# The second product of an MLP block as seven products of halves

## The chip, the cores and the metric

The kernel runs on one core of a Trainium2 chip. A core has a matrix engine (TensorE, PE in the profile; it writes its results to PSUM, eight banks of 128 partitions by 512 fp32 values), a vector engine (VectorE, DVE), a scalar engine (ScalarE, ACT), GpSimd (POOL), which here mainly issues loads, and a queue for DMA transfers (SyncE, SP). Each engine works through its own list of instructions in order and waits on semaphores for the others. The metric is the device time of one execution in microseconds (us). Before the change the median of three runs was 309.07 us (308.72 to 309.33).

## The reference

Retention attention over 8 sequences of 576 tokens with 8 heads of 64, followed by an MLP with a hard-swish:

```python
scores = scale * np.matmul(q, k.transpose(0, 1, 3, 2))
Dmat = np.where(rel >= 0, gamma ** rel, 0.0)
attn_out = np.matmul(scores * Dmat, v)
x = attn_out.transpose(0, 2, 1, 3).reshape(B * S, H * D)   # 4608 x 512
h = x @ w_in                                               # 512 x 2048
g = h * np.clip(h + 3.0, 0.0, 6.0) / 6.0
out = g @ w_out                                            # 2048 x 512, fp32 out
```

The change touches only the last line, for six of the nine blocks of tokens.

## The kernel before

**Tiling.** The 4608 tokens are cut into nine blocks of 512 (`MBLK`). Block `b` below 8 is the first 512 tokens of sequence `b`; block 8 gathers the last 64 tokens of each of the eight sequences. The attention works in pieces of 128 tokens: four main pieces per sequence, and a "rest" piece for the last 64 tokens of two sequences.

**GEMM1 of a block** (`gemm1`, `g1`, lines 402 to 410) has 16 units, one per 128 hidden features `fc`. A unit is four matmuls of 512 columns into one PSUM bank `ph`; ScalarE makes `u` from it (L409), and VectorE multiplies `u` and `ph` into `gt[:, fc, :]` (L410, f16). `gt` is the transposed `g` of the block: 128 partitions of features, 16 feature chunks, 512 tokens. There are two `gt` buffers.

**GEMM2 of a block** (`g2`, L460) also has 16 units: for each of four groups of 128 tokens (`mc`), four parts of four matmuls, with `gt` as weights and 512 columns of `wout16` moving. After the fourth part ScalarE copies the bank to `osb` (L464) and SP stores it (L445). The last group of the last block is done in two halves of 256 columns (`g2_halves`, L473).

**PSUM.** Four banks have the tag `ph` (GEMM1, GEMM2, and some attention tiles), two hold the scores `sc`, one `o`, one `u` of the states.

**The order around the change** is written out by hand (`manual_schedule`): the program text is the order of each engine. `put(units, steps)` emits the units of a GEMM and, after unit `j`, the work listed under `j`; -1 is ahead of the first. While block `kb` is in GEMM2 the attention of the pieces of block `kb + 1` is emitted in between:

- `step(ended, begun)` (lines 591 to 608): the inter-piece matmuls of the pieces that end (L325), the scores of the pieces that begin (L303 into `sc`, and L578 into two `ph` banks for the second one), then the products with v of those that end (L336, their results copied by ScalarE to `xt` at L342), and the state products of those that begin (L360). VectorE masks the scores (L307, L586) and advances the state (L373, or L376 and L377, giving `ts`); ScalarE copies `ts` into `tbd` with two copies (L389, L390).
- `ahead(c)`: transposes for the pieces of the block after the next, through SP (L288, and L294 after VectorE has scaled q and v at L293).

Blocks 2, 4 and 6 carry five pieces (one rest piece and four main pieces), blocks 1, 3 and 5 four, block 7 one. `AT` says after which units the steps come, by the number of pieces:

```python
AT = {1: (-1, 7), 4: (-1, 7, 12), 5: (-1, 3, 7, 11)}
```

GpSimd issues the loads of q, k, v (L91), six pieces ahead (`NBUF`); `load_until` in a step issues the next ones once buffers come free.

Of the kernel before, what the change touches and what calls it, by code (L numbers as in the profile page):

```python
# [10 lines left out]
FP32 = mybir.dt.float32  # L11
FP16 = mybir.dt.float16
ACTF = mybir.ActivationFunctionType
ALU = mybir.AluOpType
# [3 lines left out]
def kernel(  # L18
# [16 lines left out]
    nc = tc.nc  # L35
    B, H, S, D = q.shape
    NTOK, DM = out.shape
    DFF = moe_w_in.shape[1]
    P = 128
    NPAIR = H // 2  # L40
    HALF = P // 2
    NCC = DM // P
    NFC = DFF // P
    MBLK = 512
    NMB = NTOK // MBLK
    MAIN = MBLK
# [8 lines left out]
    for b in range(B):  # L55
# [3 lines left out]
        if b >= 2 and b % 2 == 0 or b == B - 1:  # L59
            j = (b - 1) // 2  # L60
# [2 lines left out]
    NP = len(pieces)  # L63
    lng = [float(np.log(1.0 - 2.0 ** (-5.0 - h))) for h in range(H)]

    def column_of(c):
        kind, b, i, _ = pieces[c]
        return b * MAIN + i * P if kind == "main" else B * MAIN + b * P

    const = ctx.enter_context(tc.tile_pool(name="const", bufs=1))  # L70
    big = ctx.enter_context(tc.tile_pool(name="big", bufs=1))
    nat = ctx.enter_context(tc.tile_pool(name="nat", bufs=6))
    work = ctx.enter_context(tc.tile_pool(name="work", bufs=3))
    psum = ctx.enter_context(tc.tile_pool(name="psum", bufs=1, space=bass.MemoryType.PSUM))
    ctx.enter_context(tc.manual_schedule())

    win16 = big.tile([P, NCC, DFF], FP16)
    wout16 = big.tile([P, NFC, DM], FP16)
    xt16 = big.tile([P, NCC, NTOK], FP16)

    loaded = {}
    EARLY = 4
    NBUF = 6

    def load(c):
# [29 lines left out]
    first = const.tile([P, 1], FP32)  # L115
    nc.scalar.activation(first, cb[:, 0:1], ACTF.Exp)
    lnr = const.tile([P, H], FP32)
    for h in range(H):
# [17 lines left out]
                            in1=gq[:, :, None].to_broadcast([P, H, P]), op=ALU.mult)  # L136
# [24 lines left out]
    for i in range(5):  # L161
        t = const.tile([P, NPAIR, P], FP16, name=f"tbd{i}")
        if i >= EARLY:
            nc.vector.memset(t, 0.0)
# [53 lines left out]
    def q_by_pe(c):  # L218
        q16, qk = loaded[c]["q16"], qk_of(c)
        pq = psum.tile([P, NPAIR, P], FP32, tag="ph", bufs=4, name=f"trq_{c}")  # L220
        for p in range(NPAIR):
            for h2 in range(2):
                r = slice(h2 * HALF, h2 * HALF + HALF)
                nc.tensor.matmul(pq[r, p, :], q16[:, 2 * p + h2, :], dq[:, 2 * p + h2, :],
                                 start=(p == 0), stop=(p == NPAIR - 1), skip_group_check=True)
        if c == EARLY - 1:
            for p in (0, 2):
# [22 lines left out]
    def out_last(c):  # L250
        before, qk = st[c]["before"], st[c]["qk"]
        at, vs = st[c]["at"], st[c]["vs"]
        g0 = column_of(c)
        halves = [psum.tile([P, NPAIR, P], FP32, tag="o", name=f"o_{c}"),
                  psum.tile([P, NPAIR, P], FP32, tag="ph", bufs=4, name=f"o2_{c}")]
        for i, o in enumerate(halves):
            for p in range(2):
                nc.tensor.matmul(o[:, p, :], tbd[before][:, 2 * i + p, :], qk[:, 0, 2 * i + p, :],
                                 start=(p == 0), stop=False, skip_group_check=True)
        for i, o in enumerate(halves):  # L260
            for p in range(2):
                for h2 in range(2):
                    r = slice(h2 * HALF, h2 * HALF + HALF)
                    nc.tensor.matmul(o[r, p, :], vs[:, 4 * i + 2 * p + h2, :],
                                     at[:, h2, 2 * i + p, :],
                                     start=False, stop=(p == 1), skip_group_check=True)
            nc.scalar.copy(xt16[:, 2 * i:2 * i + 2, g0:g0 + P], o[:, 0:2, :])  # L267

    def state_early(c):

# [60 lines left out]
    def intra(c, copy_later=False, more=False):  # L331
        o, at, vs = st[c]["o"], st[c]["at"], st[c]["vs"]
        for p in range(NPAIR):
            for h2 in range(2):
                r = slice(h2 * HALF, h2 * HALF + HALF)
                nc.tensor.matmul(o[r, p, :], vs[:, 2 * p + h2, :], at[:, h2, p, :],  # L336
                                 start=(st[c]["first"] and p == 0),
                                 stop=(p == NPAIR - 1 and not more), skip_group_check=True)
        g0 = column_of(c)

        def copy():
            nc.scalar.copy(xt16[:, :, g0:g0 + P], o)  # L342

        if copy_later:
            return copy
        copy()
# [50 lines left out]
    gts = {}  # L397

    def g1_mm(kb, ph, fc, dmcs):
        t0 = kb * MBLK  # L400
        for dmc in dmcs:
            nc.tensor.matmul(ph, win16[:, dmc, P * fc:P * fc + P], xt16[:, dmc, t0:t0 + MBLK],  # L402
                             start=(dmc == 0), stop=(dmc == NCC - 1))

    def g1_act(kb, ph, fc):
        if kb not in gts:
            gts[kb] = work.tile([P, NFC, MBLK], FP16, tag="gt16", bufs=2, name=f"gt16_{kb}")
        u = work.tile([P, MBLK], FP32, tag="moeu", bufs=3, name=f"u_{kb}_{fc}")
        nc.scalar.activation(u, ph, ACTF.Relu, bias=cb[:, 0:1], scale=1.0 / 6.0)  # L409
        nc.vector.scalar_tensor_tensor(out=gts[kb][:, fc, :], in0=u, scalar=1.0,  # L410
                                       in1=ph, op0=ALU.min, op1=ALU.mult)
# [8 lines left out]

    def g1_columns(kb, fc, ph, cols):

        t0 = kb * MBLK
        for dmc in range(NCC):
            nc.tensor.matmul(ph[:, cols], win16[:, dmc, P * fc:P * fc + P],  # L425
                             xt16[:, dmc, t0 + cols.start:t0 + cols.stop],
                             start=(cols.start == 0 and dmc == 0),
                             stop=(cols.stop == MBLK and dmc == NCC - 1),
                             skip_group_check=True)
        if cols.stop == MBLK:  # L430
            g1_act(kb, ph, fc)
# [10 lines left out]
    def store(kb, mc, cols, src):  # L442
        if kb < B:
            r0 = kb * S + P * mc
            nc.sync.dma_start(out[r0:r0 + P, cols], src)  # L445
        else:
            for i in range(2):
                r0 = (2 * mc + i) * S + MAIN
                queue = nc.scalar if i else nc.sync
                queue.dma_start(out[r0:r0 + HALF, cols], src[i * HALF:i * HALF + HALF])  # L450
# [3 lines left out]
    def g2(kb, mc, part):  # L454
        gt = gts[kb]
        if part == 0:
            pouts[kb, mc] = psum.tile([P, DM], FP32, tag="ph", bufs=4, name=f"pout_{kb}_{mc}")
        pout = pouts[kb, mc]
        for fc in range(4 * part, 4 * part + 4):
            nc.tensor.matmul(pout, gt[:, fc, P * mc:P * mc + P], wout16[:, fc, :],  # L460
                             start=(fc == 0), stop=(fc == NFC - 1))
        if part == 3:
            osb = work.tile([P, DM], FP32, tag="osb", bufs=4, name=f"osb_{kb}_{mc}")
            nc.scalar.copy(osb, pout)  # L464
            store(kb, mc, slice(0, DM), osb)

    def g2_halves(kb, mc):
        gt = gts[kb]
# [60 lines left out]
    def unit1(kb, f0):  # L529
        return lambda: g1(kb, f0)  # L530

    def unit2(kb, mc, part):
        return lambda: g2(kb, mc, part)
# [76 lines left out]
    def put(units, steps):  # L610

        for do, *which in steps.get(-1, ()):
            do(*which)
        for j, unit in enumerate(units):
            unit()
            run_later(1)
            for do, *which in steps.get(j, ()):
                do(*which)

    def of_block(kb):  # L620
        return list(range(last_of[kb - 1] + 1, last_of[kb] + 1)) if kb < NMB else []

    def gemm1(kb, steps):

        units = {0: [lambda: g1_first(kb)]}.get(kb, [])
        done = {0: 2, 1: 4}.get(kb, 0)
        put(units + [unit1(kb, f) for f in range(done, NFC)], steps)

    load_until(EARLY - 1 + NBUF)
    gemm1(0, {9: [(fill_gq,)]})
    order = [(mc, part) for part in range(4) for mc in range(3)] + [(3, part) for part in range(4)]
    put([unit2(0, mc, part) for mc, part in order],
        {3: [(first_step, 3)], 6: [(make_mask_rest,)], 9: [(first_step, 4)],
         11: [(first_step, 5)], 13: [(first_step, 6)], 14: [(first_step, 7), (transpose_k, 8)],
         15: [(transpose_k, 9)]})

    banks = [g1_bank(1, fc) for fc in range(4)]
    done, last = slice(0, 3 * P), slice(3 * P, MBLK)  # L640
# [4 lines left out]
    for fc, cols in ((2, done), (0, last), (1, last), (3, done), (2, last), (3, last)):  # L645
# [3 lines left out]

    gemm1(1, {0: [(transpose_q, 9)], 1: [(transpose_k, 10)],  # L650
              4: [(transpose_q, 10)], 5: [(transpose_k, 11)], 8: [(transpose_q, 11)]})
    AT = {1: (-1, 7), 4: (-1, 7, 12), 5: (-1, 3, 7, 11)}
    for kb in range(1, NMB - 1):
        mine, next_ = of_block(kb + 1), of_block(kb + 2)
        pairs = [mine[i:i + 2] for i in range(0, len(mine), 2)]
        steps = {}
        for j, ended, begun in zip(AT[len(mine)], [[]] + pairs, pairs + [[]]):
            steps.setdefault(j, []).append((step, ended, begun))
        for j, c in enumerate(next_, start=16 - len(next_)):
            steps.setdefault(j, []).append((ahead, c))  # L660
        put([unit2(kb, mc, part) for mc in range(MBLK // P) for part in range(4)], steps)
        gts.pop(kb)
        gemm1(kb + 1, {})
    for mc in range(MBLK // P - 1):
        for part in range(4):
            g2(NMB - 1, mc, part)
# [31 lines left out]
```

## Time and profile before

| | |
|---|---|
| median of three runs | 309.07 us (308.72 to 309.33) |
| profiled execution, first to last instruction (its span) | 309.9 us; the profile gives no other time for it |
| TensorE busy | 298.6 us, 2238 matmuls |
| VectorE busy | 185.2 us |
| ScalarE busy | 174.3 us |
| GpSimd busy | 109.0 us |
| GEMM2 matmuls of 512 columns (L460) | 560, 379 ns each from start to modelled end |
| GEMM2 matmuls of 256 columns (L473) | 32, 272 ns |
| block 4, GEMM2 with five pieces | 166.85 to 185.43 us |
| block 5, GEMM2 with four pieces | 199.34 to 216.91 us |
| block 7, GEMM2 with one piece | 263.30 to 278.14 us |

Matmuls are pipelined: the duration of one runs from its start to its modelled end, and the next starts earlier, so the rate is read from starts. A group's row in the profile gives its line in the kernel, engine, operation, tiles, shapes, count, then busy time and the mean of one, then the idle time of the engine ahead of it and what ended most of that. In a timeline each row is: start, duration of the merged group, engine, line, operation, tiles, shapes, count, and in brackets the idle time before it and who ended it. PEclk is the granted TensorE clock, 1.00 being full speed.

### The profile page before, as it was taken

The numbers are of one execution on the slowest core, as the hardware profiler recorded it, in microseconds if no ns is written. First come the engines' busy times: TensorE is split into PE (matmuls) and PEld (weight loads), VectorE is DVE, ScalarE is ACT, GpSimd is POOL, SyncE is SP. The second block draws the span as 40 slices with busy tenths as digits, with TensorE's granted clock in tenths as the row PEclk, the third lists the DMA queues.
The fourth block names the chain that finished last, engine by engine and source line by source line (L and its number), as shares of the span: only waits on it lengthen the run. The fifth ranks groups of instructions, "written<-read, shape, count | busy, mean of one in ns | idle before, by whom it ended". The sixth has DMA issues, their size and how long they took to land.

```text
span 309.9 us, 5776 instructions
## 1 busy us (share of the span) xinstructions
PE 298.6 (96%) x2238; PEld 150.2 (48%) x2238; DVE 185.2 (60%) x308; ACT 174.3 (56%) x301; POOL 109.0 (35%) x135
## 2 busy tenths in 40 slices
PE   5969998999999999999999999999999999999994
PEld 2634445644554554445544644455445544444443
DVE  4728616798657782885578746857688347307700
ACT  5528537685457463854475637644774567227611
POOL 8973568456522392035433650158000000000000
PEclk9779999999999999999999999999999999999999
DMA  9999999999999899629999999199930120011022
GB/s 71 144 199 203 190 146 197 130 152 148 156 173 111 110 153 174 122 17 157 149 136 114 125 167 160 18 134 151 141 87 36 68 68 2 34 68 36 1 68 68
DMA packets 153163, 35.51 MB, mean 115 GB/s; under 512 B 143792, under 2 KB 148656, under 8 KB 153136
## 3 DMA queue, kind: packets, MB, share of 16 engines
q0 software_dynamic: 117264, 18.36, 84.1%
q1 hardware_dynamic: 35472, 16.26, 26.5%
q10 hardware_dynamic: 400, 0.52, 0.5%
q8 instruction: 17, 0.28, 0.4%
q14 instruction: 10, 0.08, 0.1%
HBM read 36.70 MB, written 9.44 MB: 149 GB/s over the span
## 4 chain that ended last, share of the span: by engine, by line
PE 90%; POOL 4%; DMA 2%; ACT 2%; DVE 1%; issue 0%; POOLq 0%; ACTq 0%
PE ph L402 39%; PE pout L460 39%; PE o L336 3%; DMA qv<-in_v_dram 2%; POOL qv L91 2%; PE sc L303 2%; PE o L325 2%; PE u L360 1%; POOL kn L91 1%; PE pout L473 1%; PE sc L578 1%; PE ph L425 1%; ACT qk L216 0%; POOL vs L202 0%; ACT xt L342 0%
## 5 line engine op out<-in xcount | busy, mean ns | idle before, releaser
L410 DVE SCALAR_TENSOR_TENSOR gt<-u,ph 128x512 f16<-128x512 f32 x144 | 98.1, 687 | 67.4 <-ACT u L409 66.7
L460 PE MATMUL pout<-wout,gt 128*128 128x512 f16 x560 | 126.0, 379 | 0.0
L402 PE MATMUL ph<-xt,win 128*128 128x512 f16 x560 | 123.0, 380 | 0.5 <-ACT xt L267 0.3
L409 ACT ACTIVATE u<-ph,cb 128x512 f32<-128x512 f32 x144 | 98.3, 687 | 26.4 <-PE ph L402 25.2
L402 PEld LDWEIGHTS <-win 128*128 128x128 f16 x560 | 54.9, 98 | 66.9 <-issue 1.6
L460 PEld LDWEIGHTS <-gt 128*128 128x128 f16 x560 | 52.7, 98 | 60.8
L91 POOL DMA_DIRECT2D kn<-in_k_dram x40 | 34.4, 864 | 93.0 <-PE u L360 71.5
L464 ACT COPY osb<-pout 128x512 f32<-128x512 f32 x35 | 20.5, 586 | 48.9 <-PE pout L460 48.6
L307 DVE TENSOR_TENSOR at<-sc,mask_wide 128x1024 f16<-128x1024 f32 x19 | 23.2, 1222 | 27.2 <-PE sc L303 27.1
L91 POOL DMA_DIRECT2D qv<-in_q_dram x40 | 34.4, 866 | 5.6 <-DMA wout<-in_moe_w_out_dram 3.3
L91 POOL DMA_DIRECT2D qv<-in_v_dram x40 | 34.8, 876 | 2.9 <-DMA wout<-in_moe_w_out_dram 1.7
L389 ACT COPY tbd<-ts 64x256 f16<-64x256 f16 x28 | 11.3, 404 | 32.7 <-DVE ts L373 16.9
L342 ACT CAST xt<-o 128x512 f16<-128x512 f32 x35 | 19.4, 589 | 6.8 <-PE o L336 4.5
L293 DVE TENSOR_TENSOR vs<-qv,gqv 128x1024 f16<-128x1024 f16 x28 | 17.9, 685 | 2.9 <-DMA qv<-in_v_dram 2.9
L586 DVE TENSOR_TENSOR at<-sc,mask_wide 128x512 f16<-128x512 f32 x24 | 15.4, 681 | 0.0
L336 PE MATMUL o<-at,vs 128*64 128x128 f16 x280 | 12.4, 225 | 1.1 <-ACT xt L342 0.9
L390 ACT COPY tbd<-ts 64x256 f16<-64x256 f16 x28 | 11.2, 402 | 0.4
L336 PEld LDWEIGHTS <-vs 128*64 128x64 f16 x280 | 8.9, 111 | 4.4 <-DVE vs L202 2.1
L376 DVE TENSOR_TENSOR ta<-u,ts 128x256 f32<-128x256 f32 x21 | 8.7, 415 | 3.1 <-PE u L360 3.1
L377 DVE TENSOR_TENSOR ts<-ta,gc 128x256 f16<-128x256 f32 x21 | 8.9, 425 | 1.7
L303 PE MATMUL sc<-qk 64*128 64x128 f16 x184 | 9.4, 222 | 0.6 <-ACT qk L230 0.6
L325 PEld LDWEIGHTS <-tbd 128*128 128x128 f16 x112 | 7.0, 98 | 4.0
(70 smaller groups left out, 117.5 us busy)
## 6 DMA issues: line engine op xcount, KB each, us to landing
out_dram<-osb SPq DMA_DIRECT2D x32, 256.0 KB, 4.2
kn<-in_k_dram POOLq DMA_DIRECT2D x32, 128.0 KB, 4.4
qv<-in_q_dram POOLq DMA_DIRECT2D x32, 128.0 KB, 4.9
qv<-in_v_dram POOLq DMA_DIRECT2D x32, 128.0 KB, 5.8
wout<-in_moe_w_out_dram POOLq DMA_DIRECT2D x4, 512.0 KB, 14.7
win<-in_moe_w_in_dram POOLq DMA_DIRECT2D x3, 512.0 KB, 12.1
win<-in_moe_w_in_dram POOLq DMA_DIRECT2D x2, 256.0 KB, 8.1
kn<-in_k_dram POOLq DMA_DIRECT2D x8, 64.0 KB, 4.8
```

The source lines that it names most:

```text
L91: nc.gpsimd.dma_start(dst[p0:p0 + n], src[b, :, s0:s0 + n, :].rearrange("h s d -> s h d"))
L293: nc.vector.tensor_tensor(out=vs, in0=loaded[c]["qv"], in1=gqv, op=ALU.mult)
L303: nc.tensor.matmul(sc[:, h2, p, :], qk[r, 1, p, :], qk[r, 0, p, :], start=True, stop=True)
L307: later.append(lambda: nc.vector.tensor_tensor(out=at.rearrange("t a b s -> t (a b) s"), in0=sc.rearrange("t a b s -> t (a b) s"), in1=mas ...
L336: nc.tensor.matmul(o[r, p, :], vs[:, 2 * p + h2, :], at[:, h2, p, :], start=(st[c]["first"] and p == 0), stop=(p == NPAIR - 1 and not more ...
L342: nc.scalar.copy(xt16[:, :, g0:g0 + P], o)
L402: nc.tensor.matmul(ph, win16[:, dmc, P * fc:P * fc + P], xt16[:, dmc, t0:t0 + MBLK], start=(dmc == 0), stop=(dmc == NCC - 1))
L409: nc.scalar.activation(u, ph, ACTF.Relu, bias=cb[:, 0:1], scale=1.0 / 6.0)
L410: nc.vector.scalar_tensor_tensor(out=gts[kb][:, fc, :], in0=u, scalar=1.0, in1=ph, op0=ALU.min, op1=ALU.mult)
L460: nc.tensor.matmul(pout, gt[:, fc, P * mc:P * mc + P], wout16[:, fc, :], start=(fc == 0), stop=(fc == NFC - 1))
L464: nc.scalar.copy(osb, pout)
L586: nc.vector.tensor_tensor(out=at[:, h2], in0=banks[h2], in1=mask[:, None, :].to_broadcast([P, NPAIR, P]), op=ALU.mult)
```

## The change

For blocks 2 to 7 the product of `g` (512 x 2048) and `w_out` (2048 x 512) is split in two along tokens, features and output columns, and the eight products of halves are replaced by seven, with sums of halves on both sides (the scheme known from Strassen and Winograd, with nested sums).

- **Sums of `w_out`** (`tw1` to `tw4`, 128 x 8 x 256, f16) are made once by VectorE during GEMM2 of block 0, after units 5 to 8.
- **Sums of `g`** (`s1` to `s4`, 128 x 8 x 256, f16) are made by VectorE for every block. `s1` and `s2` are made in pieces during GEMM1, whose units now go in the order 0, 8, 1, 9, ... ; their last parts stand ahead of GEMM2, `s3` and `s4` after its units 3 and 4.
- **GEMM2** has 14 units: products 1, 2, 6, 5, 7, 3, 4, each for two groups of 128 tokens, eight matmuls of 256 columns per unit.
- **Results.** Three `ph` banks are used. Bank `b` accumulates products 1, 6, 7 and 4 in turn, and is copied to SBUF by ScalarE after 1, 6 and 7; the next product is added to what stands in it. Bank `c` does so with 5 and 3. Bank `a` holds product 2. VectorE adds two of the four output quarters, GpSimd one, ScalarE copies the fourth. Each half of 256 tokens is stored by one DMA of 512 KB.
- **Order.** `AT` has a second table for these blocks, for 14 units, and with five pieces the single one now comes first. `ahead` ends at unit 12 of 14 where it ended at 15 of 16.
- **Buffers.** One `gt` buffer in place of two; `xt` is one tile per block, two in turn, in place of one for all tokens.

```diff
+    SEVEN = 2
-            gts[kb] = work.tile([P, NFC, MBLK], FP16, tag="gt16", bufs=2, name=f"gt16_{kb}")
+            gts[kb] = work.tile([P, NFC, MBLK], FP16, tag="gt16", bufs=1, name=f"gt16_{kb}")
...
+    def combine_wout(i):
+        one, other = {1: (b12, b11), 2: (b22, tw[1]), 3: (b22, b12), 4: (b21, tw[2])}[i]
+        nc.vector.tensor_tensor(out=tw[i], in0=one, in1=other, op=ALU.subtract)
...
+    def sum_of(kb, i, q0, q1):
...
+        gt, sm, q = gts[kb], sums[kb], slice(q0, q1)
+        r = slice(half_k + q0, half_k + q1)
+        one, other, op = {1: (gt[:, q, hi], gt[:, r, hi], ALU.add),
+                          2: (sm[1][:, q], gt[:, q, lo], ALU.subtract),
+                          3: (gt[:, q, lo], gt[:, q, hi], ALU.subtract),
+                          4: (gt[:, r, lo], sm[2][:, q], ALU.subtract)}[i]
+        nc.vector.tensor_tensor(out=sm[i][:, q], in0=one, in1=other, op=op)
...
+    def product(kb, which, tt):
+        my, gt, sm = seven[kb], gts[kb], sums[kb]
+        chain, first, left, right = {
+            1: ("b", True, gt[:, lo_k, lo], b11),
+            6: ("b", False, sm[2], tw[2]),
+            7: ("b", False, sm[3], tw[3]),
+            4: ("b", False, gt[:, hi_k, hi], tw[4]),
+            2: ("a", True, gt[:, hi_k, lo], b21),
+            5: ("c", True, sm[1], tw[1]),
+            3: ("c", False, sm[4], b22)}[which]
+        if chain not in my:
+            my[chain] = psum.tile([P, 2, half_n], FP32, tag="ph", bufs=4, name=f"{chain}_{kb}")
+        for k in range(half_k):
+            nc.tensor.matmul(my[chain][:, tt], left[:, k, P * tt:P * tt + P], right[:, k, :],
+                             start=(first and tt == 0 and k == 0),
+                             stop=(k == half_k - 1), skip_group_check=True)
+
+    def gather(kb, which):
+        my = seven[kb]
+        if which in (1, 6, 7, 5):
+            my[which] = work.tile([P, 2, half_n], FP32, tag=f"part{which}", bufs=1,
+                                  name=f"part{which}_{kb}")
+            nc.scalar.copy(my[which], my["c" if which == 5 else "b"])
+        if which == 2:
+            my["lo"] = work.tile([P, 2, DM], FP32, tag="osb2", bufs=3, name=f"olo_{kb}")
+            nc.vector.tensor_tensor(out=my["lo"][:, :, lo_n], in0=my[1], in1=my["a"], op=ALU.add)
+        if which == 7:
+            my["hi"] = work.tile([P, 2, DM], FP32, tag="osb2", bufs=3, name=f"ohi_{kb}")
+            nc.gpsimd.tensor_tensor(out=my["hi"][:, :, hi_n], in0=my[7], in1=my[5], op=ALU.add)
+        if which == 3:
+            nc.vector.tensor_tensor(out=my["lo"][:, :, hi_n], in0=my[6], in1=my["c"], op=ALU.add)
+            store2(kb, 0, my["lo"])
+        if which == 4:
+            nc.scalar.copy(my["hi"][:, :, lo_n], my["b"])
+            store2(kb, 1, my["hi"])
...
+        return [unit(which, tt) for which in (1, 2, 6, 5, 7, 3, 4) for tt in range(2)]
...
-    AT = {1: (-1, 7), 4: (-1, 7, 12), 5: (-1, 3, 7, 11)}
+    AT = {False: {1: (-1, 7), 4: (-1, 7, 12), 5: (-1, 3, 7, 11)},
+          True: {1: (-1, 5), 4: (-1, 5, 12), 5: (-1, 1, 5, 12)}}
+    within = {4: [(1, 0, 2)], 8: [(1, 2, 4)], 10: [(2, 0, 4)], 12: [(1, 4, 6)]}
+    behind = {-1: [(1, 6, 8), (2, 4, 8)], 3: [(3, 0, 8)], 4: [(4, 0, 8)]}
...
+        single = len(mine) % 2 if by_seven else 0
+        pairs = [mine[:1]] * single + [mine[i:i + 2] for i in range(single, len(mine), 2)]
+        if by_seven:
+            for j, which in behind.items():
+                steps[j] = [(sum_of, kb, *w) for w in which]
...
-        for j, c in enumerate(next_, start=16 - len(next_)):
+        for j, c in enumerate(next_, start=(13 if by_seven else 16) - len(next_)):
```

More of the change, by code (lines that the diff above doesn't have):

```diff
@@ L64, with place_of @@
     lng = [float(np.log(1.0 - 2.0 ** (-5.0 - h))) for h in range(H)]
-    def column_of(c):
+    def place_of(c):
         kind, b, i, _ = pieces[c]
-        return b * MAIN + i * P if kind == "main" else B * MAIN + b * P
+        return (b, i * P) if kind == "main" else (B, b * P)
     const = ctx.enter_context(tc.tile_pool(name="const", bufs=1))
@@ L72 @@
     nat = ctx.enter_context(tc.tile_pool(name="nat", bufs=6))
+    xpool = ctx.enter_context(tc.tile_pool(name="xpool", bufs=2))
     work = ctx.enter_context(tc.tile_pool(name="work", bufs=3))
@@ L78, with xt_of @@
     wout16 = big.tile([P, NFC, DM], FP16)
-    xt16 = big.tile([P, NCC, NTOK], FP16)
+    xts = {}
+    def xt_of(kb):
+        if kb not in xts:
+            if kb == B:
+                xts[kb] = big.tile([P, NCC, MBLK], FP16, name="xt_rest")
+            else:
+                xts[kb] = xpool.tile([P, NCC, MBLK], FP16, tag="xt", name=f"xt_{kb}")
+        return xts[kb]
     loaded = {}
     EARLY = 4
+    SEVEN = 2
     NBUF = 6
@@ L252, in out_last @@
         at, vs = st[c]["at"], st[c]["vs"]
-        g0 = column_of(c)
+        kb, g0 = place_of(c)
         halves = [psum.tile([P, NPAIR, P], FP32, tag="o", name=f"o_{c}"),
@@ L266, in out_last @@
                                      start=False, stop=(p == 1), skip_group_check=True)
-            nc.scalar.copy(xt16[:, 2 * i:2 * i + 2, g0:g0 + P], o[:, 0:2, :])
+            nc.scalar.copy(xt_of(kb)[:, 2 * i:2 * i + 2, g0:g0 + P], o[:, 0:2, :])
     def state_early(c):
@@ L338, in intra @@
                                  stop=(p == NPAIR - 1 and not more), skip_group_check=True)
-        g0 = column_of(c)
+        kb, g0 = place_of(c)
         def copy():
-            nc.scalar.copy(xt16[:, :, g0:g0 + P], o)
+            nc.scalar.copy(xt_of(kb)[:, :, g0:g0 + P], o)
         if copy_later:
@@ L399, in g1_mm @@
     def g1_mm(kb, ph, fc, dmcs):
-        t0 = kb * MBLK
         for dmc in dmcs:
-            nc.tensor.matmul(ph, win16[:, dmc, P * fc:P * fc + P], xt16[:, dmc, t0:t0 + MBLK],
+            nc.tensor.matmul(ph, win16[:, dmc, P * fc:P * fc + P], xt_of(kb)[:, dmc, :],
                              start=(dmc == 0), stop=(dmc == NCC - 1))
@@ L421, in g1_columns @@
     def g1_columns(kb, fc, ph, cols):
-        t0 = kb * MBLK
         for dmc in range(NCC):
             nc.tensor.matmul(ph[:, cols], win16[:, dmc, P * fc:P * fc + P],
-                             xt16[:, dmc, t0 + cols.start:t0 + cols.stop],
+                             xt_of(kb)[:, dmc, cols],
                              start=(cols.start == 0 and dmc == 0),
@@ L465, in g2 @@
             store(kb, mc, slice(0, DM), osb)
+    half_k, half_t, half_n = NFC // 2, MBLK // 2, DM // 2
+    lo_k, hi_k = slice(0, half_k), slice(half_k, NFC)
+    lo, hi = slice(0, half_t), slice(half_t, MBLK)
+    lo_n, hi_n = slice(0, half_n), slice(half_n, DM)
+    tw = {i: big.tile([P, half_k, half_n], FP16, name=f"tw{i}") for i in range(1, 5)}
+    b11, b12 = wout16[:, lo_k, lo_n], wout16[:, lo_k, hi_n]
+    b21, b22 = wout16[:, hi_k, lo_n], wout16[:, hi_k, hi_n]
+    def combine_wout(i):
+        one, other = {1: (b12, b11), 2: (b22, tw[1]), 3: (b22, b12), 4: (b21, tw[2])}[i]
+        nc.vector.tensor_tensor(out=tw[i], in0=one, in1=other, op=ALU.subtract)
@@ new lines @@
+    sums = {}
+    def sum_of(kb, i, q0, q1):
+        if kb not in sums:
+            sums[kb] = {j: work.tile([P, half_k, half_t], FP16, tag=f"s{j}", bufs=1,
+                                     name=f"s{j}_{kb}") for j in range(1, 5)}
+        gt, sm, q = gts[kb], sums[kb], slice(q0, q1)
[5 more added lines that the diff above has]
+        nc.vector.tensor_tensor(out=sm[i][:, q], in0=one, in1=other, op=op)
@@ new lines @@
+    seven = {}
+    def product(kb, which, tt):
[14 more added lines that the diff above has]
+                             stop=(k == half_k - 1), skip_group_check=True)
@@ L467, in g2_halves, with store2, gemm2_seven, unit @@
+    def store2(kb, i, src):
+        r0 = kb * S + half_t * i
+        nc.sync.dma_start(out[r0:r0 + half_t, :].rearrange("(t p) n -> p t n", p=P), src)
+    def gemm2_seven(kb):
+        seven[kb] = {}
+        def unit(which, tt):
+            def do():
+                product(kb, which, tt)
+                if tt == 1:
+                    gather(kb, which)
+            return do
+        return [unit(which, tt) for which in (1, 2, 6, 5, 7, 3, 4) for tt in range(2)]
     def g2_halves(kb, mc):
@@ L625, in gemm1 @@
         units = {0: [lambda: g1_first(kb)]}.get(kb, [])
-        done = {0: 2, 1: 4}.get(kb, 0)
-        put(units + [unit1(kb, f) for f in range(done, NFC)], steps)
+        if kb < SEVEN or kb == NMB - 1:
+            rest = range({0: 2, 1: 4}.get(kb, 0), NFC)
+        else:
+            rest = [f for q in range(half_k) for f in (q, q + half_k)]
+        put(units + [unit1(kb, f) for f in rest], steps)
     load_until(EARLY - 1 + NBUF)
@@ L633 @@
     order = [(mc, part) for part in range(4) for mc in range(3)] + [(3, part) for part in range(4)]
[L634 to L637, printed above, removed]
+    steps = {3: [(first_step, 3)], 6: [(make_mask_rest,)], 9: [(first_step, 4)],
+             11: [(first_step, 5)], 13: [(first_step, 6)],
+             14: [(first_step, 7), (transpose_k, 8)], 15: [(transpose_k, 9)]}
+    for j, i in zip((5, 6, 7, 8), (1, 2, 3, 4)):
+        steps.setdefault(j, []).append((combine_wout, i))
+    put([unit2(0, mc, part) for mc, part in order], steps)
     banks = [g1_bank(1, fc) for fc in range(4)]
@@ L651 @@
               4: [(transpose_q, 10)], 5: [(transpose_k, 11)], 8: [(transpose_q, 11)]})
-    AT = {1: (-1, 7), 4: (-1, 7, 12), 5: (-1, 3, 7, 11)}
+    AT = {False: {1: (-1, 7), 4: (-1, 7, 12), 5: (-1, 3, 7, 11)},
+          True: {1: (-1, 5), 4: (-1, 5, 12), 5: (-1, 1, 5, 12)}}
+    within = {4: [(1, 0, 2)], 8: [(1, 2, 4)], 10: [(2, 0, 4)], 12: [(1, 4, 6)]}
+    behind = {-1: [(1, 6, 8), (2, 4, 8)], 3: [(3, 0, 8)], 4: [(4, 0, 8)]}
     for kb in range(1, NMB - 1):
+        by_seven = kb >= SEVEN
         mine, next_ = of_block(kb + 1), of_block(kb + 2)
-        pairs = [mine[i:i + 2] for i in range(0, len(mine), 2)]
+        single = len(mine) % 2 if by_seven else 0
+        pairs = [mine[:1]] * single + [mine[i:i + 2] for i in range(single, len(mine), 2)]
         steps = {}
-        for j, ended, begun in zip(AT[len(mine)], [[]] + pairs, pairs + [[]]):
+        if by_seven:
+            for j, which in behind.items():
+                steps[j] = [(sum_of, kb, *w) for w in which]
+        for j, ended, begun in zip(AT[by_seven][len(mine)], [[]] + pairs, pairs + [[]]):
             steps.setdefault(j, []).append((step, ended, begun))
-        for j, c in enumerate(next_, start=16 - len(next_)):
+        for j, c in enumerate(next_, start=(13 if by_seven else 16) - len(next_)):
             steps.setdefault(j, []).append((ahead, c))
-        put([unit2(kb, mc, part) for mc in range(MBLK // P) for part in range(4)], steps)
+        put(gemm2_seven(kb) if by_seven else
+            [unit2(kb, mc, part) for mc in range(MBLK // P) for part in range(4)], steps)
         gts.pop(kb)
-        gemm1(kb + 1, {})
+        gemm1(kb + 1, {j: [(sum_of, kb + 1, *w) for w in which] for j, which in within.items()}
+              if SEVEN <= kb + 1 < NMB - 1 else {})
     for mc in range(MBLK // P - 1):
```

## The prediction

> **What bounds the kernel now.** I read the page first: the busy line, the chain that ended last, the costliest groups.
>
> ```profile
> PE 298.6 (96%) x2238; PEld 150.2 (48%) x2238; DVE 185.2 (60%) x308; ACT 174.3 (56%) x301; POOL 109.0 (35%) x135
> ...
> PE 90%; POOL 4%; DMA 2%; ACT 2%; DVE 1%; issue 0%; POOLq 0%; ACTq 0%
> ...
> L460 PE MATMUL pout<-wout,gt 128*128 128x512 f16 x560 | 126.0, 379 | 0.0
> ...
> L464 ACT COPY osb<-pout 128x512 f32<-128x512 f32 x35 | 20.5, 586 | 48.9 <-PE pout L460 48.6
> ```
>
> TensorE is the bound: 96% busy, 90% of the chain, and no idle time ahead of L460. The edit takes TensorE columns away and gives VectorE and ScalarE work, so two questions decide: what is a 256-column matmul worth, and do two engines at 60% and 56% stay out of TensorE's way? The last block answers the first, since it has both shapes (timeline, TensorE alone: start, us, count).
>
> ```profile
> 291.95 10.52 PE L460 MATMUL pout<-wout,gt 128*128 128x512 f16 x48
> 302.31 3.66 PE L473 MATMUL pout<-wout,gt 128*128 128x256 f16 x32
> ```
>
> 48 wide matmuls take 302.31-291.95 = 10.36 us, 216 ns each. The 32 narrow ones, each with new weights, take 3.66 less the last one's own 0.272, over 31 starts: 109 ns. So the weight load stays hidden at half width. For the second question I read the timeline of one GEMM2 phase, block 5's, which starts with the scores at S = 199.34.
>
> ```profile
> 199.34 0.40 PE L303 MATMUL sc<-qk 64*128 64x128 f16 x8
> ...
> 200.26 7.08 PE L460 MATMUL pout<-wout,gt 128*128 128x512 f16 x32
> ...
> 200.77 1.22 DVE L307 TENSOR_TENSOR at<-sc,mask_wide 128x1024 f16<-128x1024 f32 x1
> ...
> 201.90 0.41 DVE L373 TENSOR_TENSOR ts<-u,gc 128x256 f16<-128x256 f32 x1
> 202.24 1.28 DVE L586 TENSOR_TENSOR at<-sc,mask_wide 128x512 f16<-128x512 f32 x2
> ...
> 203.88 0.42 DVE L377 TENSOR_TENSOR ts<-ta,gc 128x256 f16<-128x256 f32 x1
> ...
> 204.34 0.41 ACT L389 COPY tbd<-ts 64x256 f16<-64x256 f16 x1 [1.17 <-DVE ts L377]
> 204.75 0.40 ACT L390 COPY tbd<-ts 64x256 f16<-64x256 f16 x1
> ...
> 205.18 0.59 ACT L464 COPY osb<-pout 128x512 f32<-128x512 f32 x1
> ...
> 207.18 0.39 PE L325 MATMUL o<-qk,tbd 128*128 128x128 f16 x4
> ```
>
> The first output bank is complete at 200.26 + 16 x 0.216 = 203.7, but its copy runs at 205.18: ScalarE works in order, and the state copies ahead of it wait for ts, the end of a step's VectorE work. Today that costs nothing, as TensorE goes on in another bank. In the new scheme TensorE itself waits for that copy.
>
> **TensorE's saving.** Per block 64 x 0.2158 = 13.81 us become 112 x 0.1093 = 12.24: 1.57 less. The three phase types last, from their first scores to the next GEMM1, 18.58 us (five pieces; 166.85 to 185.43), 17.56 (four; 199.34 to 216.91) and 14.84 (one; 263.30 to 278.14). With attention costed by the same rows the phases without a wait would be 16.87 (one step's pairing also changes), 15.97 and 13.16. Six blocks: 3 x 1.71 + 2 x 1.59 + 1.68 = 10.0 us.
>
> **VectorE's new work.** Sums are two-input f16 operations inside SBUF. The nearest row is L293 (128x1024, 685 ns, 0.60 from start to start), and L202 (128x512, 419); so 0.42, 0.69 and 0.685 + 0.533 = 1.22 for 512, 1024 and 2048 elements. The upper bound is one element per cycle, as L135 shows (1.226 for 1024, one input repeated): 0.69, 1.22, 2.29. I take the lower: the sums' rows are contiguous over 256 elements as L293's are. The Trainium skill's "VectorE: DVE Perf Modes" (What auto-detection actually checks) asks for 16-bit types with step one; L293's 685 ns agrees, and no run here shows the strided case yet.
>
> In GEMM1 a VectorE unit is 0.69 of 0.863 us, so the four pieces of sums there (1.9 us) fit; their largest backlog is about 0.35 us, and a bank has about 1.0 to spare: nothing. The four sums of halves of w_out in block 0 (4.6 us) fall where VectorE waits 8.32 us for the scores; the last w_out load lands near 41.9, so they end near 45.4, just as L307 starts at 45.53: nothing, at worst 0.3.
>
> **Four-piece phases (3 and 5), times after S.** GEMM1's last gt is written at 1.52 (200.16 + 0.69). Then the last parts of s1 and s2, one dependent on the other, delay the first mask from 1.43 to 2.74. Masks and states keep their own row distances, so the second ts ends at 6.27 (204.30 - 199.34 + 1.31). ScalarE: two state copies to 7.12, then the copy of product 1's bank to 7.74. TensorE: scores and updates 0.92, products 1 and 2 to 4.42, and product 6 may not start before 7.78: **3.36 us idle**. Behind the copy hangs VectorE's queue: add of a and product 1 (0.59 effective, as L586), s3 and s4 (1.14 each), and only at 10.65 the second pair's mask; its states end at 14.76 (the step's rows, 207.94 to 212.09, are 4.1 us). ScalarE: state copies to 15.6, then the copy of product 5 to 16.22. Product 3 starts at 16.26 where TensorE, even after waiting 0.7 for a bank, stood ready at 15.4. Products 3 and 4 and the last step: 16.26 + 3.50 + 1.11 = 20.87. The xt copies then have one unit (0.875) to hide in instead of three and need 0.96 + 0.05 (214.19 + 1.07 - 214.31): 0.14 more. End 21.01 against 17.56: +3.45.
>
> **Five-piece phases (2, 4 and 6).** The single piece comes first; step 1 needs the one sc bank for the next scores, and its mask ends at 2.74 + 1.22 = 3.96, while TensorE is there at 2.3: 1.7 idle. Then VectorE's queue: masks and states to 7.94, add 8.53, s3 and s4 to 10.81, masks and states to 14.92; ScalarE's state copies to 15.77, product 5's copy to 16.38. Product 3 waits 1.65 for it. End: 16.42 + 3.50 + 1.11 + 0.14 = 21.17 against 18.58: +2.59.
>
> **Phase 7** has one piece; every copy is early, -1.68.
>
> ScalarE loses four output copies a block (0.586 each, L464) and gains five of that size; VectorE gains two adds (0.68 each, as L586) and the sums. In the phases above these are counted where they stand in the queues; their share of busy time plays no part.
>
> Sum: 3 x 2.59 + 2 x 3.45 - 1.68 = +13.0 us.
>
> **Queues and the rest.** SP: the transposes begin at unit 8 of 14 with one store among them that waits for the add of product 3, and ten of them at 1.3 us still end some 7 us before the next phase. POOL's add (1.15 by L202 on POOL) stands behind loads; only a store waits for it, with three output buffers. One gt buffer costs nothing: TensorE has read the old one before the first new bank is full.
>
> **The clock.** The trace shows what gaps do (one-us windows, TensorE: us, busy, granted clock, DMA):
>
> ```profile
> 5.00:6.00 1.00, 0.65 (x5) 1.00 2.07 132
> 6.00:7.00 1.00, 0.21 (x8) 1.00 2.29 146
> 7.00:8.00 1.00, 0.64 (x14) 1.00 2.31 147
> 8.00:9.00 1.00, 1.00 (x17) 0.79 2.25 143
> 9.00:10.00 1.00, 1.00 (x14) 0.50 2.06 131
> ```
>
> After three us about half idle, with no gap over 1.14 us, the clock is at 0.50 for three us. A gap of 3.36 us should do that in each four-piece phase. It doubles product 6 and the step after it, up to 1.7 us, of which VectorE's lead over the next scores (10.22 against 10.65) and the wait before product 3 take some: +1.0 each (bounds 0 and 1.7), 2.0 in all. The 1.7 us gaps of the five-piece phases leave a stretch half busy with dense matmuls; I take no drop.
>
> The Trainium skill's "TensorE: Matmul & The Clock Gate" (Part 1: The HAM clock gate) ties the drop to a whole idle window of about 3.4 us. By that rule 3.36 us would not do and the sum would stay at +13.0; the trace shows a drop without such a window.
>
> Total +15.0. The profiled span, 309.9, is 0.8 above the median of the runs, 309.07; the difference goes onto the median: **324.1 us**.
>
> **Rivals.**
> - *No clock drop*: +13.0, 322.1.
> - *Drops in the five-piece phases too*: after the first gap about 0.9 (product 2 comes late to the add), after the second up to 1.65 straight on the end: 3 x 2.55 = 7.7 more, 331.8. For it: the windows above. Against: those held small matmuls with longer pauses.
> - *Sums at one element per cycle*: (0.27 + 0.53) + 2 x 1.07 = 2.9 us more per phase in VectorE's queue, five phases: 322.1 + 14.7 = 336.8. Against: L293.
> - *Faster: the copy of the gathered bank is in time.* If ScalarE got to product 1's copy at 2.9 (bank full) instead of 7.1, and the adds and sums cleared likewise, only 10.0 less remains: 299.1. It decides where the waits come to less than 1.6 us a phase; in the row above a copy already runs 1.3 us late behind the states with no sums in the queue, which speaks against it.
>
> **Numbers.** 324.1: 0.42; 322.1: 0.25; 331.8: 0.19; 336.8: 0.08; 299.1: 0.05; 0.01 for anything near no change. Two runs here differ by up to 0.2%, about what can be told from no change. Range 317 to 335: it holds the first three cases, and small errors in VectorE's distances (5% of 13 us in five phases, 3.3 us).
>
> **What would show it.** Product matmuls 109 ns apart; product 6 in phases 3 and 5 waiting about 3.4 us for ScalarE's copy, which follows two state copies; in 2, 4 and 6 the second scores waiting 1.7 us for VectorE; product 3 waiting 0.8 to 1.7 us for the copy of product 5; phases of 21 to 22 us; sums of 1.22 us; a granted clock below 1 in the new phases. I am wrong if ScalarE's copies come out of this order, if sums cost double, or if the clock drops on every gap.

## The result and the profile after

| | before | after |
|---|---|---|
| median of four runs | 309.2 us (308.72 to 311.68) | 324.86 us (322.44 to 326.01) |
| profiled execution: span, time | 309.9 us; 311.7 us if the same 1.8 lies around it as after (the highest of the four runs took 311.68) | 324.2 us; 326.01 us |
| ratio | | 1.0473, 95% interval 1.0404 to 1.0541 |

The kernel is 4.7% slower. The page of the changed kernel, the busy line and the chain that ended last by engine and by line:

```profile
PE 293.4 (90%) x2526; PEld 179.6 (55%) x2526; DVE 225.0 (69%) x372; ACT 177.5 (55%) x307; POOL 116.7 (36%) x141
...
PE 68%; DVE 17%; ACT 6%; POOL 3%; issue 2%; DMA 2%; DVEq 0%; POOLq 0%; ACTq 0%
PE ph L412 38%; PE pout L469 11%; PE b L520 7%; PE c L520 4%; DVE at L318 4%; DVE at L679 4%; DVE s L502 4%; PE o L347 2%; DMA qv<-in_v_dram 2%; POOL qv L102 2%; DVE ts L388 2%; DVE ta L387 2%; DVE gt L420 1%; ACT u L419 1%; ACT part L530 1%
```

TensorE is busy for 5 us less and still the kernel takes longer: 17% of the chain is now VectorE's and 6% ScalarE's, where they had 1% and 2%. The waits of TensorE name the places (engine, line, for whom: total us, times, longest):

```profile
PE b L520 <- ACT part L530: 6.1, 2, 3.1
PE c L520 <- ACT part L530: 5.4, 5, 1.7
PE sc L314 <- DVE at L318: 4.2, 3, 1.4
PE c L520 <- ACT xt L353: 3.5, 5, 0.7
```

The first is product 6 in phases 3 and 5, the second product 3 in five phases, the third the scores in phases 2, 4 and 6, the fourth the bank of product 5. In phase 4, which starts with the scores at S = 173.66, the second scores and product 3 look like this (TensorE's timeline):

```profile
173.66 0.40 PE L314 MATMUL sc<-qk 64*128 64x128 f16 x8
...
177.55 0.40 PE L314 MATMUL sc<-qk 64*128 64x128 f16 x8 [1.40 <-DVE at L318]
...
189.97 1.91 PE L520 MATMUL c<-wout,s 128*128 128x256 f16 x16 [1.66 <-ACT part L530]
```

The GEMM2 phases, from their first scores to the next GEMM1, from the timelines (us):

| phase | pieces | before | predicted | after |
|---|---|---|---|---|
| 2, 4, 6 | five | 18.58 each | 21.17 | 21.04, 21.05, 21.04 |
| 3, 5 | four | 17.56, 17.57 | 22.0 with the clock drop | 22.15, 21.95 |
| 7 | one | 14.84 | 13.16 | 13.25 |

Together they are 14.8 us longer; the spans differ by 14.3. In phase 5 the wait for the bank and what holds it up look like this (timeline of the changed kernel, TensorE, ScalarE and VectorE; S = 208.61):

```profile
209.54 1.92 PE L520 MATMUL b<-wout,gt 128*128 128x256 f16 x16
211.29 1.91 PE L520 MATMUL a<-wout,gt 128*128 128x256 f16 x16
216.27 2.77 PE L520 MATMUL b<-tw,s 128*128 128x256 f16 x16 [3.07 <-ACT part L530]
218.84 0.63 PE L336 MATMUL o<-qk,tbd 128*128 128x128 f16 x4
...
212.81 0.41 ACT L400 COPY tbd<-ts 64x256 f16<-64x256 f16 x1 [3.40 <-DVE ts L384]
213.24 0.40 ACT L401 COPY tbd<-ts 64x256 f16<-64x256 f16 x1
214.79 0.40 ACT L400 COPY tbd<-ts 64x256 f16<-64x256 f16 x1 [1.16 <-DVE ts L388]
215.21 0.40 ACT L401 COPY tbd<-ts 64x256 f16<-64x256 f16 x1
215.63 0.58 ACT L530 COPY part<-b 128x512 f32<-128x512 f32 x1
...
216.31 0.69 DVE L533 TENSOR_TENSOR olo<-part,a 128x512 f32<-128x512 f32 x1 [1.55 <-ACT part L530]
216.91 1.22 DVE L502 TENSOR_TENSOR s<-gt 128x2048 f16<-128x2048 f16 x1
```

Product 1's 16 matmuls are issued in 211.29 - 209.54 = 1.75 us, 109 ns each, and its bank is full near 211.5. The copy runs at 215.63, behind four state copies that wait for VectorE. Product 6 starts at S + 7.66. It then takes 218.84 - 216.27 = 2.57 us instead of 1.75, since the clock has dropped (same phase by one-us windows: us, busy TensorE, PEld, VectorE, ScalarE, GpSimd, granted clock, DMA):

```profile
215.00:216.00 1.00, 0.00 (x0) 0.00 (x0) 0.00 (x0) 0.96 (x3) 0.03 (x1) 1.00 2.38 152
216.00:217.00 1.00, 0.73 (x7) 0.66 (x7) 0.69 (x2) 0.22 (x1) 0.00 (x0) 1.00 2.39 152
217.00:218.00 1.00, 1.00 (x8) 0.73 (x7) 1.00 (x1) 0.00 (x0) 0.00 (x0) 0.57 1.29 82
218.00:219.00 1.00, 1.00 (x7) 0.75 (x6) 1.00 (x2) 0.00 (x0) 0.00 (x0) 0.50 0.15 21
219.00:220.00 1.00, 1.00 (x17) 0.80 (x16) 0.27 (x1) 0.59 (x1) 0.00 (x0) 0.50 0.00 0
220.00:221.00 1.00, 1.00 (x32) 0.80 (x28) 0.94 (x1) 0.10 (x1) 0.00 (x0) 0.72 0.00 0
```

### The profile page after: what moved, and what is told of

Read it like the earlier page. It is cut to its first block, busy times and chain, and to the rows that moved or that the text cites. A ratio compares the mean times of both kernels' runs of the same rounds, so it can differ in the third digit from the quotient of the medians.

```text
span 324.2 us, 6404 instructions
## 1 busy us (share of the span) xinstructions
PE 293.4 (90%) x2526; PEld 179.6 (55%) x2526; DVE 225.0 (69%) x372; ACT 177.5 (55%) x307; POOL 116.7 (36%) x141
## 4 chain that ended last, share of the span: by engine, by line
PE 68%; DVE 17%; ACT 6%; POOL 3%; issue 2%; DMA 2%; DVEq 0%; POOLq 0%; ACTq 0%
PE ph L412 38%; PE pout L469 11%; PE b L520 7%; PE c L520 4%; DVE at L318 4%; DVE at L679 4%; DVE s L502 4%; PE o L347 2%; DMA qv<-in_v_dram 2%; POOL qv L102 2%; DVE ts L388 2%; DVE ta L387 2%; DVE gt L420 1%; ACT u L419 1%; ACT part L530 1%
## 5 line engine op out<-in xcount | busy, mean ns | idle before, releaser
L412 PE MATMUL ph<-xt,win 128*128 128x512 f16 x496 | 109.5, 382 | 0.5 <-ACT xt L278 0.3
L520 PEld LDWEIGHTS <-s 128*128 128x128 f16 x384 | 38.4, 100 | 21.6 <-issue 16.1
L469 PE MATMUL pout<-wout,gt 128*128 128x512 f16 x176 | 39.6, 379 | 0.0
L520 PE MATMUL b<-tw,s 128*128 128x256 f16 x192 | 25.3, 290 | 6.1 <-ACT part L530 6.1
L520 PEld LDWEIGHTS <-gt 128*128 128x128 f16 x288 | 27.1, 98 | 4.0
L400 ACT COPY tbd<-ts 64x256 f16<-64x256 f16 x28 | 11.3, 404 | 31.6 <-DVE ts L388 21.1
L469 PEld LDWEIGHTS <-gt 128*128 128x128 f16 x176 | 16.7, 98 | 19.1
L530 ACT COPY part<-b 128x512 f32<-128x512 f32 x18 | 10.6, 587 | 16.5 <-PE b L520 16.4
L502 DVE TENSOR_TENSOR s<-gt 128x512 f16<-128x512 f16 (+1 forms) x30 | 17.4, 580 | 0.2
L520 PE MATMUL c<-wout,s 128*128 128x256 f16 x96 | 11.4, 272 | 5.4 <-ACT part L530 5.4
L473 ACT COPY osb<-pout 128x512 f32<-128x512 f32 x11 | 6.4, 585 | 17.0 <-PE pout L469 16.9
```

Of the source, the lines that this page charges most:

```text
L412: nc.tensor.matmul(ph, win16[:, dmc, P * fc:P * fc + P], xt_of(kb)[:, dmc, :], start=(dmc == 0), stop=(dmc == NCC - 1))
L502: nc.vector.tensor_tensor(out=sm[i][:, q], in0=one, in1=other, op=op)
L520: nc.tensor.matmul(my[chain][:, tt], left[:, k, P * tt:P * tt + P], right[:, k, :], start=(first and tt == 0 and k == 0), stop=(k == half_ ...
L530: nc.scalar.copy(my[which], my["c" if which == 5 else "b"])
```

## The experiments

The theory: TensorE's saving is whole, but in-order queues of VectorE and ScalarE (sums, masks, state copies, then the copies of the gathered banks) hold TensorE up, and its long gaps cost clock. The rivals: the sums come late by themselves; the clock has no part in it; the new buffers cost something.

All times are medians with the kernel before beside them on the same chip, at 309.8 us in the first four and 309.7 in the last four. Executions of one kernel differ by up to 4.5 us (308.9 to 313.4 for the kernel before), and the profiles differ ahead of phase 2 as well: the loading stage has clock drops that fall at different places (0.79 from 16 to 24 us in the profile of the changed kernel, 1.00 throughout in that with the gap filled), and phase 2 begins between 100.0 and 103.3 us. Phases are therefore compared by their lengths.

**The saving alone.** The seven products only in phase 7:

```diff
-    SEVEN = 2
+    SEVEN = 7
```

> The seven products in phase 7 alone, where one piece of attention runs beside them; blocks 2 to 6 as before the change, but with the single gt buffer, the new xt tiles and the four sums of w_out kept. Theory: the phase loses its 1.6 us and nothing else changes: 309.2 - 1.6 = 307.6 us. Rival, the buffers or the sums of w_out cost something by themselves: 309 us or more.

307.59 us, ratio 0.9937 (0.9911 to 0.9963). Phase 7 is 13.25 us long, against 14.84; the other phases are as before (18.58 and 17.57). So the saving of 1.6 us is there, and buffers and the sums of w_out cost nothing that shows.

**State copies of the first step behind the copy of product 1**, phases 3 and 5 only. The copies are kept in a list and issued after unit 1:

```diff
+        if hold:
+            held.append(copies)
...
+            hold = by_seven and begun and (len(mine), j) in ((4, -1),)
+            steps.setdefault(j, []).append((step, ended, begun, hold))
+            if hold:
+                steps.setdefault({-1: 1}[j], []).append((release,))
```

> Only in phases 3 and 5 (four pieces): the four state copies of the first step are issued on ScalarE behind the copy of product 1's bank instead of ahead of it. Queue theory: the bank copy then runs about 2.9 us after the scores start, product 6 starts at 4.4 without its 3.1 us wait and without a clock drop behind it. But VectorE's queue then sets product 3: sums to 9.1, states to 13.3, two state copies and the copy of product 5 to 14.7, so product 3 waits about 2.6 us where it waited 0.2. Phases 3 and 5 go from 22.1 to 19.5 us: 324.9 - 5.2 = 319.7 us, up to 322 if the new wait brings a clock drop. Rival, the sums alone keep product 6 waiting (s2 late): no change, 324.9.

320.6 us, ratio 1.0358 (1.0313 to 1.0403). Product 6 no longer waits at all; product 3 waits 2.25 us instead of 0.24 and 0.15, in both phases (TensorE's timeline of this kernel, phase 3, then phase 5):

```profile
142.65 1.91 PE L528 MATMUL b<-tw,s 128*128 128x256 f16 x16
...
152.82 3.09 PE L528 MATMUL c<-wout,s 128*128 128x256 f16 x16 [2.25 <-ACT part L538]
155.70 1.57 PE L528 MATMUL b<-tw,gt 128*128 128x256 f16 x8
...
212.49 1.91 PE L528 MATMUL b<-tw,s 128*128 128x256 f16 x16
...
222.66 1.91 PE L528 MATMUL c<-wout,s 128*128 128x256 f16 x16 [2.25 <-ACT part L538]
224.40 1.04 PE L528 MATMUL b<-tw,gt 128*128 128x256 f16 x8
```

The order of ScalarE's queue was the cause of the first wait, and s2 was not late. More than half of the wait came back further down, as forecast. The two phases do the same with the same wait, but last 21.00 and 19.33 us: in phase 3 the wait was followed by a clock drop (2.88 us for product 3), in phase 5 not (1.74). One-us windows of TensorE in this kernel (us, busy, clock, DMA):

```profile
154.00:155.00 1.00, 1.00 (x6) 0.50 0.54 108
...
223.00:224.00 1.00, 1.00 (x12) 1.00 0.63 126
```

**State copies of the later step behind the copy of product 5**, five phases:

```diff
+            hold = by_seven and begun and (len(mine), j) in ((4, 5), (5, 5))
...
+                steps.setdefault({5: 7}[j], []).append((release,))
```

> Only the step after unit 5, in the five phases with attention: its state copies are issued on ScalarE behind the copy of product 5's bank (after unit 7) instead of ahead of it. Queue theory: product 3 finds its bank copied; the waits of 1.66 us in phases 2, 4 and 6 and of 0.2 us in phases 3 and 5 go: 324.9 - 5.0 - 0.4 = 319.5 us; the waits for the scores (1.4 us) and for product 6 (3.1 us) stay. Rival, product 3 waits for s4 from VectorE: no change.

317.81 us, ratio 1.0279 (1.0232 to 1.0325). Phases 2, 4 and 6 last 19.29 us instead of 21.04, phases 3 and 5 21.74 and 21.56: 6.1 us less. The two profiled executions differ by 8.7 us (326.01 and 317.35); the rest of that is the start, as phase 2 begins at 100.05 instead of 102.66. Whether an earlier start is also why the median lies below the 319.5 expected is not shown. Product 3 starts as soon as product 7 is issued (TensorE, phase 4):

```profile
181.63 1.91 PE L528 MATMUL b<-tw,s 128*128 128x256 f16 x16
183.38 1.91 PE L528 MATMUL c<-wout,s 128*128 128x256 f16 x16
```

s4 was there in time; the wait for the scores (1.41 us) and the one for product 6 (3.1) stayed.

**The gap filled with work.** 14 matmuls of zeros ahead of product 2 in phases 3 and 5:

```diff
+        if which == 2 and tt == 0 and kb in (3, 5):
+            for _ in range(14):
+                nc.tensor.matmul(my[chain].rearrange("p a b -> p (a b)"), zeros[:, 0:P], zeros,
+                                 start=True, stop=True, skip_group_check=True)
```

> Extra work: in phases 3 and 5, 14 matmuls of zeros with 512 columns (3.0 us) into bank a ahead of product 2, whose first matmul clears it, so that TensorE is busy where it waited for the copy of product 1. Clock theory: the granted clock stays at 1.00 in both phases, product 6 takes 1.75 us instead of 2.6 to 3.3, the phases last 21.0 us instead of 22.0, and the spread between runs (322.4 to 326.0) shrinks to its lower end: 322 to 323 us in spite of 6 us more TensorE work. Rival, the clock has no part in it: 324 to 326 us with the same spread.

321.66 us (321.43 to 322.31), ratio 1.0385 (1.035 to 1.042). The phases last 20.90 and 21.00 us instead of 22.15 and 21.95 (timeline, phase 5, and both phases by window):

```profile
208.16 3.19 PE L521 MATMUL a<-zeros 128*128 128x512 f16 x14
211.18 1.91 PE L524 MATMUL a<-wout,gt 128*128 128x256 f16 x16
213.13 1.91 PE L524 MATMUL b<-tw,s 128*128 128x256 f16 x16
214.88 0.39 PE L336 MATMUL o<-qk,tbd 128*128 128x128 f16 x4
...
135.73:156.63 20.90, 19.50 (x235) 15.52 (x235) 16.45 (x26) 8.31 (x17) 11.78 (x13) 1.00 1.25 92
205.47:226.47 21.00, 19.52 (x236) 15.55 (x235) 16.46 (x26) 8.31 (x17) 10.63 (x13) 1.00 1.22 88
```

More work made the phases shorter by 1.1 us each: that is the price of the clock drop, against 1.0 in the prediction. Product 3 waits 0.66 and 0.75 us here, where it waited 0.24 and 0.15: the slow clock had been hidden in part in that wait. Another 1.9 us of the gain lies in the start (phase 2 begins at 100.78), so the narrower spread between runs is not shown to come from the filled gap.

**The sums' share.** The sums of g are not computed:

```diff
-        nc.vector.tensor_tensor(out=sm[i][:, q], in0=one, in1=other, op=op)
+        return
...
+        sm = {1: gt[:, lo_k, hi], 2: gt[:, lo_k, hi], 3: gt[:, lo_k, lo], 4: gt[:, hi_k, lo]}
```

> The changed kernel without the sums of g: s1 to s4 are left out and products 6, 5, 7 and 3 take halves of gt in their place (so this part of the computation is missing); instruction order otherwise as in the changed kernel. Prices VectorE's sums alone: the masks start 1.3 us earlier and the second pair's 2.3 us earlier. Queue theory: phases 3 and 5 19.3 us, phases 2, 4 and 6 18.5 us, 310 to 311 us in all; the waits behind the state copies that are left still cost the whole saving. Rival, the sums are the whole loss: 299 to 301 us.

311.19 us, ratio 1.0047 (1.0016 to 1.0077); phases 18.50 and 19.30 us. Of the 4.2 us by which a five-piece phase is longer than the estimate without waits (21.04 against 16.87), the sums account for 2.5. The four-piece phases are 2.8 us shorter than in the changed kernel, of which about 1.1 is the clock drop, which is absent here; product 6 still waits 1.88 us in both for its copy behind the state copies.

**Both moves of copies together:**

> Both moves of state copies together (first step in phases 3 and 5, step after unit 5 in phases 2 to 6). Queue theory: no product waits for a bank's copy any more; phases 3 and 5 last 17.0 us (16.0 of work, 0.7 for bank c, the xt copies), phases 2, 4 and 6 19.3 us with their 1.4 us for the scores and 0.7 for bank c. From 321.7 us (the kernel with the gap filled, its phases 21.0): -4.0 x 2 - 1.75 x 3 = 308.4 us, level with the kernel before. Rival, the two moves together only pass the wait on to the sums s3 and s4: 313 us or more.

310.06 us where 308.4 was expected, ratio 1.0029 (1.0005 to 1.0053). The five-piece phases last 19.29 us as expected, the four-piece ones 17.58 where 17.0 was. The expectation that no product waits any more was wrong by one: the held state copies are released behind product 5's copy but ahead of product 7's, so product 4 waits (ScalarE and TensorE of this kernel, phase 5):

```profile
212.97 0.40 ACT L407 COPY tbd<-ts 64x256 f16<-64x256 f16 x1
213.40 0.58 ACT L538 COPY part<-b 128x512 f32<-128x512 f32 x1
...
214.03 1.03 PE L528 MATMUL b<-tw,gt 128*128 128x256 f16 x8 [0.50 <-ACT part L538]
```

**The first mask ahead of the tails of s1 and s2**, where the first step has one piece:

```diff
+                if j >= 0 or len(mine) == 4:
+                    steps[j] = [(sum_of, kb, *w) for w in which]
...
+        if by_seven and len(mine) != 4:
+            steps[-1] += [(sum_of, kb, *w) for w in behind[-1]]
```

> As the one with both moves, and in phases 2, 4, 6 and 7 the last parts of s1 and s2 are issued on VectorE behind the first step's mask instead of ahead of it. Queue theory: the mask ends 1.3 us earlier, so the scores of the next step wait 0.1 to 0.4 us instead of 1.4: phases 2, 4 and 6 last 18.2 us, 308.4 - 3 = 305.4 us. Rival, the sums then come late to product 6: no gain or a loss against 308.4.

307.93 us where 305.4 was expected, ratio 0.9938 (0.9916 to 0.996). The scores wait 0.2 us instead of 1.4, and the five-piece phases last 18.58 us. The expected 18.2 was missed by the same wait of product 4, 0.39 us.

**Products in the order 1, 2, 6, 7, 5, 4, 3:**

```diff
-        return [unit(which, tt) for which in (1, 2, 6, 5, 7, 3, 4) for tt in range(2)]
+        return [unit(which, tt) for which in (1, 2, 6, 7, 5, 4, 3) for tt in range(2)]
...
-        if which == 7:
+        if which == 5:
             my["hi"] = work.tile([P, 2, DM], FP32, tag="osb2", bufs=3, name=f"ohi_{kb}")
...
-                steps.setdefault({-1: 1, 5: 7}[j], []).append((release,))
+                steps.setdefault({-1: 1, 5: 9}[j], []).append((release,))
```

> As the one before, and the products in the order 1, 2, 6, 7, 5, 4, 3, so that bank c is first needed one product later (GpSimd's add moves behind product 5). Queue theory: the wait of 0.7 us for bank c goes in five phases: 305.4 - 3.4 = 302 us, close to the 299 us of the matmuls' saving alone. Rival, product 7 then waits for s3: 304 us or more.

302.56 us (302.13 to 303.13), ratio 0.9768 (0.9741 to 0.9794): 2.3% faster than the kernel before. The phases last 17.29 to 17.51 us with five pieces and 16.41 with four, 0.4 to 0.6 above what was worked out without a wait. The gain over the kernel before this one is 5.4 us, not the 3.4 expected: besides the wait for bank c, product 4's wait of 0.4 to 0.5 us went too. That 302 was hit is in part luck: the base was 2.5 us too low and the gain 2 us too small. Busy line, and phase 5 of TensorE:

```profile
PE 288.9 (96%) x2526; PEld 178.0 (59%) x2526; DVE 226.9 (76%) x372; ACT 177.7 (59%) x307; POOL 117.2 (39%) x141
...
198.10 1.91 PE L528 MATMUL b<-tw,s 128*128 128x256 f16 x16
...
201.61 1.92 PE L528 MATMUL b<-tw,s 128*128 128x256 f16 x16
203.36 1.91 PE L528 MATMUL c<-tw,s 128*128 128x256 f16 x16
205.11 1.91 PE L528 MATMUL b<-tw,gt 128*128 128x256 f16 x16
206.86 1.04 PE L528 MATMUL c<-wout,s 128*128 128x256 f16 x8
```

No product has a wait; the second scores of the five-piece phases still wait 0.2 us, and the next GEMM1 up to 0.2 us for the copies to `xt`. VectorE is busier (76%) than in the slow version (69%), with the same work (226.9 and 225.0 us) in less time. In the first order the sums cost 2.5 us of a five-piece phase; in this one they are all still there, and TensorE does not wait for the products' banks. The order decided, not the amount.

## Why the prediction was right

- **The matmul rate.** 109 ns from the last block's rows held for every product at full clock, and the saving of phase 7, which has no waits, was 1.59 us (1.68 predicted). The five other phases had waits, so their part of the saving is seen only once the order is changed.
- **Prices of the sums.** 417 to 420, 684 to 693 and 1217 to 1221 ns against 0.42, 0.69 and 1.22: the halves, rows of 256 elements at a stride, run as the contiguous rows do. That agrees with the Trainium skill's "VectorE: DVE Perf Modes" (What auto-detection actually checks), which asks for 16-bit operands with step one. The rival with doubled sums is out. The pieces of sums beside GEMM1 cost nothing, as predicted: between the GEMM2 phases of blocks 4 and 5 it takes 13.90 us (194.71 to 208.61), against 13.91 before (185.43 to 199.34).
- **Product 6 behind the state copies.** Predicted to start at S + 7.78 after 3.36 us idle, measured S + 7.66 in both phases after 3.07. The move of four copies removed the wait.
- **Scores behind the mask.** Predicted at S + 4.0, measured 177.55 - 173.66 = 3.89, with a wait of 1.40 us where 1.7 was predicted; a change of VectorE's order alone cut the wait to 0.2.
- **Product 3 behind product 5's copy.** Predicted at S + 16.42 with five pieces, measured 189.97 - 173.66 = 16.31.
- **The clock.** Predicted 1.0 us in each four-piece phase, measured 1.1 by the filled gap, and none in the five-piece phases, as taken. The drop, and that the wait before product 3 takes up part of it, were forecast; that the size came out so near is in part luck, as 1.0 was a choice between 0 and 1.7. The drop came after idle times of 3.07 us (every time) and 2.25 us (one time of two). The rule that the Trainium skill's "TensorE: Matmul & The Clock Gate" (Part 1: The HAM clock gate) states, a whole idle window of about 3.4 us, would have left the clock alone, so here the measurement decides against it.
- **What was off.** The step from span to median: I took the 0.8 us between the profiled span of 309.9 and the median as what a run differs by. About 1.8 us lies around a span (326.01 against 324.2), so the profiled execution of before took about 311.7, 2.5 above its median; its trace has two clock drops in the loading stage, near 9 and 19 us. Span against span the change is +14.3, median against median +15.7; +15.0 was predicted. The phases add up to +14.8, with errors that partly cancel: the five-piece ones 0.13 us shorter than predicted each, phase 7 0.09 longer.
- **The faster rival** named the right point: once the copies are in time and the order of the products follows, the time is 302.6, against the 299.1 without any wait.

## What to carry to other kernels

When TensorE has to wait for a copy out of a bank before it may go on in the same bank, that copy is on the critical path, and everything ahead of it in its engine's queue is too: look at what those instructions wait for, not at how long they take. Before giving up an algorithm that saves work on the bound engine, move the non-urgent instructions (here state copies, which TensorE reads only in the next step) behind the urgent ones, and reorder the products so that each copy has a whole product to hide behind. A wait of TensorE can cost more than its length (here 1.1 us more, behind a wait of 3.07).

## What the runs showed of the hardware that was not expected

The same wait of 2.25 us in two phases of one execution was followed by a half clock in one and by none in the other, so the length alone does not decide. In the profiled executions, waits of 1.4, 1.7 and 1.9 us were never followed by a drop; the waits of 3.1 us in phases 3 and 5 always were (four of four, in the changed kernel and in the one with the later copies moved). All five drops behind a wait lasted 3.4 us, worked out as twice what the one-us windows miss to a clock of 1.00: in phase 5 above, 2 x (0.43 + 0.50 + 0.50 + 0.28) = 3.42. At half clock that is 1.7 us of work at most; the two phases with the wait of 2.25 us differ by 21.00 - 19.33 = 1.67. Where the limit lies, and what else it depends on, was not tried.
